# Fewer Strassen pairs in the second layer: two groups in 10 chunks, one group in 13, chosen by the chunk ahead

## The chip, the cores and the metric

One core of one Trainium2 chip runs the program. The metric is the device time of one execution in microseconds, the median of several executions. Lower is better.

## The reference, cut to what matters

For each of four batches an attention over channels gives a 256 x 256 matrix, which is multiplied with `v`; the 24320 rows that come out go through two dense layers with a squared ReLU between them. Only the second half matters for the change:

```
def _moe_ref(x, w_in, w_out):      # x: 24320 x 256, w_in: 256 x 2048, w_out: 2048 x 256
    h = x @ w_in
    r = np.maximum(h, 0.0)
    g = r * r
    return (g @ w_out).astype(np.float32)
```

## The kernel before, in words

**Tiling.** The attention matrix of a batch is folded into `w_in`, so the first layer takes `v` itself. The 6080 columns of a batch are cut into 6 chunks of 2 x 512 columns (the last of 2 x 480), 24 chunks in all. The 2048 hidden rows are 8 quads (`j` = 0 to 7): a quad is a 2 x 2 block of tiles, two halves of the hidden rows by two halves of the chunk's columns. Every value is split into a high and a low fp32r part, and a product is three matmuls (high-high, low-high, high-low).

**First layer.** A quad takes seven products (Strassen-Winograd), 21 matmuls into PSUM banks `h`, `x` and `z` (`product`, L624). ScalarE copies partial sums from bank to bank (`m1` L667, `m6` L676, `m7` L689) and VectorE adds (`plus_m7`, L694). `block` (L640 to L645) makes the squared ReLU of the tiles "11" and "12" and splits it; `blocks` (L654 to L656) does the same for "21" and "22" together.

**Second layer.** A quad that is not paired takes 8 units of three matmuls, 24 in all (`layer2`, L755). Two neighbouring quads 2g and 2g+1 (group g) can be taken as one pair by seven products. Two of these are in `pair_unit` (L799, 12 matmuls for the pair), and five in `pair_product` (L838, 30 matmuls): 42 in place of 48. For them VectorE makes sums of tiles (`right_op`, 8 instructions at L806), and ScalarE and VectorE split four of them into high and low (`pair_split`, L813 and L814), into the one buffer `th`. The tiles "12" of a paired quad are not split in `block`. The results are added up in four tiles `res`: the first pair of a chunk starts its PSUM bank afresh; a later one gets the sum so far copied into the bank ahead of it (`pair_seed`, L822), and where a chunk has two groups, every product of the first is copied out (L852).

**Which quads.** `SGS = (0, 2)` and `groups(ci)`: no group in chunk 0, groups 0 and 2 in chunks 1 to 22, group 0 in chunk 23: 45 pairs. The pair's products come 2.6 to 5.6 quads after its first quad, so those of group 2 end in the first two quads of the next chunk. The factors of the pairs lie in scratch memory (`wss`); they are made in chunk 0 (`decode_w_out`, `combine_w_out`) and loaded on the SP queue (`load_wss`, L202). Quads that aren't paired load `wo` (`load_wo`, L197).

**Side work.** While a batch's chunks run, the next batch's scores are computed (`score_norm`, `score_split`, `score_burst`, L256, about 0.8 pairs of tiles in a quad for 30 quads), then its softmax, then the folding of its attention matrix into `w_in` (`right7`, `fold7`, L482) and the split of the result (`combine`, L538 and L539), which is written to scratch memory (L541) and read back for each quad (`load_wt`, L547). This goes on in chunks 0 to 17. `combine` writes into a buffer of `wt` (three, shared with `load_wt`) or into `th`.

**Order.** Everything is emitted in an order written out by hand: `plan` lists 15 places in a quad, and `at(u, fn, ...)` puts a piece of side work at the time u, counted in quads. `pinned` holds side work behind certain copies and adds of the main work, and `high_priority` puts an instruction ahead on its engine. Each engine takes its instructions in that order.

Of the kernel before, what the change touches and what calls it, by code (L numbers as in the profile page):

```python
# [20 lines left out]
def tile_channel_attention_relu2_ffn(ctx, tc, kq, vT, tau, w_in, w_out, outT):  # L21
# [15 lines left out]
    nc = tc.nc  # L37
# [6 lines left out]
    NJ = DFF // P // 2  # L44
# [4 lines left out]
    G = 4  # L49
# [30 lines left out]
    K12, KS4, K11, KS2, KS3, K22, KS1 = range(NP)  # L80
# [1 line left out]
    wo = {}  # L82
    ws = {}
    wosc = {}
    SGS = (0, 2)
    wss = {g: scratch.tile([P, NP, 2, 2, P], F32, name=f"wss{g}") for g in SGS}
    wo32 = scratch.tile([P, 4, C], F32, name="wo32")

# [57 lines left out]
    def decode_w_out(g):  # L146
# [15 lines left out]
        for i in range(2):  # L162
# [3 lines left out]
            nc.gpsimd.dma_start(out=wosc[j], in_=w[i].bitcast(F32))  # L166
            if g in SGS:
                for k, f, e in ((K12, 1, 0), (K11, 0, 0), (K22, 1, 1)):
                    nc.gpsimd.dma_start(out=wss[g][:, k, i], in_=w[i][:, :, f, e].bitcast(F32))
        if g == 0:  # L170
            nc.gpsimd.dma_start(out=wo32, in_=W)
        elif g in SGS:
            win["out", g] = W
# [337 lines left out]
    def combine(b, g):  # L511

        if (b, g) not in parts:
            parts[b, g] = combine_parts(b, g)
        next(parts[b, g], None)

    def combine_parts(b, g):

        eng = nc.vector
        u = us.pop((b, g))  # L520
        S = work.tile([P, 4, GW], F32, name="sq", tag="sq")
        s2, s3, s1, s4 = (S[:, i] for i in range(4))
        eng.tensor_add(out=s1, in0=u[:, 0, 1], in1=u[:, 1, 1])
        eng.tensor_sub(out=s2, in0=s1, in1=u[:, 0, 0])
        eng.tensor_sub(out=s3, in0=u[:, 0, 0], in1=u[:, 0, 1])
        eng.tensor_sub(out=s4, in0=u[:, 1, 0], in1=s2)
        for i in range(2):
            j = 2 * g + i
            if i and b:
                yield  # L530
            if b and (g, i) in ((0, 1), (3, 0)):
                w = work.tile([P, 4 * HMAX], F32R, name="th", tag="th", bufs=1)
                w = w[:, :2 * NP * P].rearrange("p (l i c) -> p l i c", l=2, i=NP)
            else:
                w = work.tile([P, 2, NP, P], F32R, name="wt", bufs=WB)
            js = slice(i * P, (i + 1) * P)
            for o, x in ((w[:, :, 0:2], u[:, :, 0, js]), (w[:, :, 2:3], u[:, 1:2, 1, js]), (w[:, :, 3:7], S[:, :, js])):
                nc.scalar.copy(out=o[:, 0], in_=x)  # L538
                eng.tensor_sub(out=o[:, 1], in0=x, in1=o[:, 0])  # L539
            wsc[b, j] = scratch.tile([P, 2, NP, P], F32, name=f"wsc{j}", bufs=2)  # L540
            nc.gpsimd.dma_start(out=wsc[b, j], in_=w.bitcast(F32))  # L541
            if b == 0:
                wt[0, j] = w
# [8 lines left out]
    chunks = [(b, 2 * sum(widths[:i]), w) for b in range(B) for i, w in enumerate(widths)]  # L552
# [43 lines left out]
    state = {}  # L596
# [3 lines left out]
    raw2 = {}  # L600

    def groups(ci):
        return () if ci == 0 else SGS[:1] if ci == len(chunks) - 1 else SGS

    def paired(q):
        return q[1] // 2 in groups(q[0])
# [12 lines left out]
    def product(q, i, out, start):  # L619
        ci, j = q  # L620
        T = chunks[ci][2]
        w, v = wt[ci, j], vt[ci, i]
        for n, (l, r) in enumerate(((0, 0), (0, 1), (1, 0))):
            nc.tensor.matmul(out=out[:, :T], lhsT=w[:, l, i], rhs=v[:, r, :T], start=start and n == 0,  # L624
                             stop=n == 2, skip_group_check=True)

    def block(q, c, ps, eng):

        T = chunks[q[0]][2]
        split = not paired(q) or c == "11"  # L630
        if paired(q):
            p, i = (q[0], q[1] // 2), q[1] % 2
            raw, tag = (raw11, "raw11") if c == "11" else (raw12, "raw12")
            if i == 0:
                raw[p] = work.tile([P, 2, HMAX], F32, name=tag, tag=tag, bufs=1)
            r = raw[p][:, i, :T]
        else:
            r = work.tile([P, HMAX], F32, name="r", bufs=1)[:, :T]
        with tc.high_priority():
            nc.scalar.activation(out=r, in_=ps[:, :T], func=AF.Relu)  # L640
        nc.scalar.activation(out=r, in_=r, func=AF.Square)  # L641
        if split:
            hl = work.tile([P, 2, HMAX], F32R, name="g1", bufs=3)
            eng(out=hl[:, 0, :T], in_=r)  # L644
            nc.vector.tensor_sub(out=hl[:, 1, :T], in0=r, in1=hl[:, 0, :T])  # L645
            gs[q, c] = hl[:, 0], hl[:, 1]
# [31 lines left out]

    def m2(q):
        product(q, A12, state[q]["X"], False)  # L680
        block(q, "11", state[q]["X"], nc.scalar.copy if q[0] == 0 and q[1] < NJ - 1 else nc.vector.tensor_copy)

    def m7(q):
        T = chunks[q[0]][2]
# [100 lines left out]
    sums2 = {}  # L785
# [30 lines left out]
    PLACE = {K11: (0, 0), KS2: (1, 0), KS3: (0, 1), KS1: (1, 1)}  # L816
    seeds = {}

    def pair_seed(p, k):
        T = chunks[p[0]][2]  # L820
        seeds[p, k] = x = ps_x.tile([P, HMAX], F32, name="x")
        nc.scalar.copy(out=x[:, :T], in_=sums2[(p[0],) + PLACE[k]][:, :T])  # L822

    def pair_product(p, k):

# [61 lines left out]
    for kt in range(NT):  # L887
        g = kt // G
# [57 lines left out]
    def at(u, fn, *args):  # L946
        side.setdefault(round(u, 3), []).append((fn, args))
# [7 lines left out]
    for g in range(1, NG):  # L955
        u = 2 * (g - 1)
# [8 lines left out]
        at(u + 1.9, decode_w_out, g)  # L965
        if g in SGS:
            at(u + 2.6, combine_w_out, g)
# [7 lines left out]
    for b in range(1, B):  # L975
        u0 = (b - 1) * QB
        first, last = (NJ + 2 if b == 1 else 0), 30
        for i in range(NT // 2):
            u, k = u0 + first + i * (last - first) // (NT // 2), 2 * i
            if k % G == 0:  # L980
                at(u - (2.15 if b > 1 and k // G == 2 else 3.4), score_load, b, k // G)
            at(u - 0.8, score_norm, b, k)
            if b > 1 or k > LATE[-1]:
                at(u - 1.0, score_split, b, k)
                at(u - 0.5, score_split, b, k + 1)
                at(u + MID, score_burst, b, [k, k + 1])
        end = u0 + last
        at(end - 0.6, squares_split, b)
        at(end + MID, norms_wide, b)
        at(end + 1.6, lambda b=b: exps(b, s_acc[b]))  # L990
        at(end + 2 + MID, attnT, b)
        for g in range(0, NG, 2):
            u = end + 3 + 3.5 * g
            if b == 1:
                at(u - 3.5, load_wins2, g)
            for i in range(NP):
                at(u + i - (0.7 if b == 1 else 2.5), right7, b, g, i)
                at(u + i + MID, fold7, b, g, i)
            for i, du in enumerate(((0, 1.78, 2, 3.55), (0, 1.55, 2.78, 3.55))[g // 2]):
                at(u + NP + du, combine, b, g + i // 2)  # L1000
    for n, (ci, j) in enumerate(quads):
        if ci:
            at(n - 1.5, load_wt, ci, j)
            if not paired((ci, j)):
                at(n - (1.0 if j // 2 - 1 not in groups(ci) else 0.7 if j % 2 else 1.7), load_wo, ci, j)
            elif j % 2 == 0:
                p = ci, j // 2
                for u, *args in ((-1.1, K12, 2), (0.85, K11), (1.8, KS2), (2.8, K22), (3.75, KS3), (4.1, KS1)):
                    at(n + u, load_wss, p, *args)
                for u, k in ((1.1, KS3), (1.2, KS1), (1.75, KS2), (1.85, K22)):  # L1010
                    at(n + u, right_op, p, k, 0)
                for u, k in ((2.15, KS3), (2.25, KS1), (2.45, KS2), (2.8, K22)):
                    at(n + u, right_op, p, k, 1)
                for u, k in ((2.95, KS2), (3.7, K22), (4.05, KS3), (4.78, KS1)):
                    at(n + u, pair_split, p, k)
                for u, k in ((2.6, K11), (3.53, KS2), (3.93, K22), (4.6, KS3), (5.6, KS1)):
                    if p[1] and k != K22:
                        at(int(n + u) + 0.4, pair_seed, p, k)
                    at(n + u, pair_product, p, k)
        if j == 0 and ci:  # L1020
            at(n - NJ + (0.05 if ci > 1 else 1.0), load_v, ci)

            def start(ci=ci, n=n):
                for k, step in enumerate(v_combos(ci)):
                    at(n + (-3.2, -2.9, -2.4, -0.95, -0.85, -0.6, -0.55)[k], v_split, *step)
            at(n - 4.0, start)
# [23 lines left out]
    for n, q in enumerate(quads):  # L1050
        if paired(q) and q[1] % 2 == 0:
            a, b = quads[n - 2], quads[n - 1]
# [11 lines left out]
    for n in range(len(quads) + 1):  # L1064
        q = quads[n] if n < len(quads) else None
# [39 lines left out]
```

## Time and profile before

| | |
|---|---|
| median of 3 runs | 2178.41 us (2176.2 to 2179.84) |
| profiled execution, its own time | 2174.31 us |
| span of its instructions | 2172.5 us |
| TensorE matmul (PE) | 2129.8 us busy, 98%, 9622 matmuls |
| TensorE weight load (PEld) | 1735.9 us, 80% |
| VectorE (DVE) | 2005.1 us, 92% |
| ScalarE (ACT) | 1603.0 us, 74% |
| DMA | 482.88 MB, mean 222 GB/s |
| granted TensorE clock | 1.000 |

PE's busy time is modelled: matmuls overlap, and a matmul that starts a little late still leaves PE busy. The number of matmuls in a stretch, each with the time from one start to the next, tells more than the busy share.

### The profile page before, as it was taken

Reading aid. Unit: us, or ns where it says so; the run is one execution under the profiler, and the core shown is the slowest. Engines: PE = TensorE matmul, PEld = TensorE weight load, DVE = VectorE, ACT = ScalarE, POOL = GpSimd, SP = SyncE. Lnnn points to the kernel's source line nnn. Section 1 sums busy time; section 2 is a strip of 40 time slices with the busy share of each in tenths; the row PEclk is TensorE's granted clock in tenths of the full one; section 3 lists DMA queues with packets and bytes.
Section 4 is the critical chain, followed back from the end, with each engine's and each line's share of the span. In section 5 each row is a group of like instructions: output and inputs, shape, how many; then the busy total and the mean of one; then the engine's idle time right before and its main releaser. Section 6 shows DMA issues by size and latency. Waiting matters only on the chain.

```text
span 2172.5 us, 27874 instructions
## 1 busy us (share of the span) xinstructions
PE 2129.8 (98%) x9622; PEld 1735.9 (80%) x9622; DVE 2005.1 (92%) x2877; ACT 1603.0 (74%) x2628; POOL 97.5 (4%) x178
## 2 busy tenths in 40 slices
PE   9999999999999999999999999999999999999999
PEld 8887787878868788887887878887777788888888
DVE  7899999999999999998999999999899898988885
ACT  6888787767777777776777777877677677677674
POOL 0120000001000000000000000000000000000000
PEclk9999999999999999999999999999999999999999
DMA  9887746467776565556867656556675665565552
GB/s 369 333 290 282 269 174 220 153 238 250 275 266 233 200 208 194 184 190 211 282 236 267 232 189 222 174 196 199 211 263 207 254 205 170 190 220 175 180 190 89
DMA packets 122045, 482.88 MB, mean 222 GB/s; under 512 B 14192, under 2 KB 16880, under 8 KB 115120
## 3 DMA queue, kind: packets, MB, share of 16 engines
q1 hardware_dynamic: 105024, 409.97, 55.6%
q0 software_dynamic: 16880, 71.12, 8.2%
q8 instruction: 77, 1.26, 0.2%
q14 instruction: 64, 0.52, 0.1%
HBM read 408.95 MB, written 72.09 MB: 221 GB/s over the span
## 4 chain that ended last, share of the span: by engine, by line
PE 78%; issue 9%; ACT 6%; DVE 5%; DMA 2%; POOL 1%; SPq 0%; POOLq 0%; ACTq 0%
PE o L755 20%; PE h L624 19%; PE z L624 10%; PE x L838 10%; PE x L624 5%; PE o L799 4%; PE h L256 3%; PE o L838 3%; PE x L256 2%; PE o L256 1%; PE h L482 1%; DMA wt<-wsc 1%; ACT raw L640 1%; DVE g L656 1%; DVE raw L806 1%
## 5 line engine op out<-in xcount | busy, mean ns | idle before, releaser
L624 PE MATMUL h<-vt,wt 128*128 128x512 f32 (+1 forms) x2304 | 632.1, 390 | 15.0 <-DMA wt<-wsc 6.1
L755 PE MATMUL o<-g,wo 128*128 128x512 f32 (+1 forms) x2352 | 613.3, 389 | 3.0 <-DVE g L644 1.9
L624 PEld LDWEIGHTS h<-vt,wt 128*128 128x128 f32 x2304 | 428.5, 188 | 114.0 <-ACT x L667 11.8
L755 PEld LDWEIGHTS o<-g,wo 128*128 128x128 f32 x2352 | 437.3, 188 | 98.0 <-DVE g L656 4.2
L624 PE MATMUL z<-vt,wt 128*128 128x512 f32 (+1 forms) x1152 | 331.4, 393 | 3.3 <-ACT z L676 3.0
L806 DVE TENSOR_TENSOR raw<-raw,raw 128x512 f32<-128x512 f32 (+1 forms) x360 | 244.0, 679 | 25.8 <-ACT raw L641 23.8
L624 PEld LDWEIGHTS z<-vt,wt 128*128 128x128 f32 x1152 | 208.7, 188 | 55.7 <-ACT z L676 16.8
L813 ACT CAST th<-raw 128x1024 fp32r<-128x1024 f32 (+1 forms) x180 | 187.8, 1043 | 69.6 <-PE x L838 39.2
L814 DVE TENSOR_TENSOR th<-raw,th 128x1024 fp32r<-128x1024 f32 (+1 forms) x180 | 217.4, 1208 | 16.4 <-ACT th L813 15.7
L838 PE MATMUL x<-th,ws 128*128 128x512 f32 (+1 forms) x810 | 212.9, 393 | 3.9 <-ACT x L822 3.3
L852 ACT COPY res<-x 128x512 f32<-128x512 f32 (+1 forms) x111 | 64.8, 584 | 180.6 <-PE x L838 167.9
L838 PEld LDWEIGHTS x<-th,ws 128*128 128x128 f32 x810 | 148.3, 188 | 44.6 <-ACT x L822 10.9
L624 PE MATMUL x<-vt,wt 128*128 128x512 f32 (+1 forms) x576 | 162.2, 388 | 0.0
L799 PE MATMUL o<-g,wo 128*128 128x512 f32 (+1 forms) x540 | 156.9, 391 | 3.3 <-ACT g L655 3.3
L645 DVE TENSOR_TENSOR g<-r,g 128x512 fp32r<-128x512 f32 (+1 forms) x204 | 138.4, 678 | 13.5 <-ACT g L644 13.0
L656 DVE TENSOR_TENSOR g<-s,g 128x1024 fp32r<-128x1024 f32 (+1 forms) x102 | 123.4, 1210 | 24.8 <-ACT g L655 23.4
L676 ACT COPY z<-h 128x512 f32<-128x512 f32 (+1 forms) x192 | 111.0, 578 | 32.0 <-PE h L624 30.4
L667 ACT COPY x<-h 128x512 f32<-128x512 f32 (+1 forms) x192 | 110.7, 576 | 32.1 <-PE h L624 30.4
L641 ACT ACTIVATE r<-r 128x512 f32<-128x512 f32 (+1 forms) x204 | 128.7, 631 | 3.1
L624 PEld LDWEIGHTS x<-vt,wt 128*128 128x128 f32 x576 | 108.1, 188 | 22.1
L654 DVE SCALAR_TENSOR_TENSOR s<-s 128x1024 f32<-128x1024 f32 (+1 forms) x102 | 122.9, 1205 | 0.1
L656 DVE TENSOR_TENSOR g<-raw,g 128x1024 fp32r<-128x1024 f32 (+1 forms) x90 | 109.0, 1211 | 14.7 <-ACT g L655 14.3
(213 smaller groups left out, 3313.7 us busy)
## 6 DMA issues: line engine op xcount, KB each, us to landing
wt<-wsc SPq DMA_DIRECT2D x184, 896.0 KB, 5.4
ws<-wss SPq DMA_DIRECT2D x225, 256.0 KB, 2.8
kqt<-kq SPq DMA_DIRECT2D x47, 1024.0 KB, 7.2
wo<-wosc SPq DMA_DIRECT2D x94, 512.0 KB, 4.3
wsc<-wt POOLq DMA_DIRECT2D x26, 896.0 KB, 6.9
wo<-wss SPq DMA_DIRECT2D x45, 512.0 KB, 4.3
v<-vT SPq DMA_DIRECT2D x40, 512.0 KB, 5.6
outT<-res POOLq DMA_DIRECT2D x80, 256.0 KB, 5.4
```

The costliest lines, as they stand in the source:

```text
L256: ins = nc.tensor.matmul(out=s[:, h * C:(h + 1) * C], lhsT=l, rhs=r, start=first and h == 0 and n == 0, stop=last and n == len(terms) - 1, ...
L624: nc.tensor.matmul(out=out[:, :T], lhsT=w[:, l, i], rhs=v[:, r, :T], start=start and n == 0, stop=n == 2, skip_group_check=True)
L641: nc.scalar.activation(out=r, in_=r, func=AF.Square)
L645: nc.vector.tensor_sub(out=hl[:, 1, :T], in0=r, in1=hl[:, 0, :T])
L654: nc.vector.scalar_tensor_tensor(out=s, in0=s, scalar=0.0, op0=ALU.max, in1=s, op1=ALU.mult)
L656: nc.vector.tensor_sub(out=l, in0=s, in1=h)
L755: nc.tensor.matmul(out=ps[:, lo:hi], lhsT=w2[:, l, f, e], rhs=r[:, lo:hi], start=start and k == 0, stop=stop and k == 2, skip_group_check= ...
L799: nc.tensor.matmul(out=o[:, :T], lhsT=w[:, l], rhs=r[:, :T], start=first and i == 0, stop=False)
L806: op(out=x, in0=x, in1=y)
L813: nc.scalar.copy(out=h, in_=x)
L814: nc.vector.tensor_sub(out=l, in0=x, in1=h)
L838: nc.tensor.matmul(out=ps[:, :T], lhsT=w[:, l], rhs=r, start=fresh and i + n == 0, stop=k != K22 and i == 1 and n == 2, skip_group_check=n ...
```

## The change

Group 1 becomes possible beside 0 and 2. A list `TWICE` names ten chunks that keep groups 0 and 2 (1, 8, 9, 14, 15 and 18 to 22); a chunk right behind one of them that isn't in the list takes group 0 alone (2, 10, 16, 23), and the nine others take group 1 alone (3 to 7, 11 to 13, 17). Besides: in the first five chunks of `TWICE` the high part of tile "11" is cast on ScalarE in place of VectorE; `combine` puts the odd quad of every group into `th`, at times evenly spaced; seeds are for group 2 alone, earlier and with priority; one split and one product of a pair come 0.12 quads later; and one load of scores comes 1.25 quads sooner.

```diff
-    SGS = (0, 2)
+    SGS = (0, 1, 2)
+    TWICE = (1, 8, 9, 14, 15, *range(18, 23))
...
-            if b and (g, i) in ((0, 1), (3, 0)):
+            if b and i:
                 w = work.tile([P, 4 * HMAX], F32R, name="th", tag="th", bufs=1)
...
     def groups(ci):
-        return () if ci == 0 else SGS[:1] if ci == len(chunks) - 1 else SGS
+        return () if ci == 0 else (0, 2) if ci in TWICE else (0,) if ci - 1 in TWICE else (1,)
...
-        block(q, "11", state[q]["X"], nc.scalar.copy if q[0] == 0 and q[1] < NJ - 1 else nc.vector.tensor_copy)
+        block(q, "11", state[q]["X"], nc.scalar.copy if q[0] == 0 and q[1] < NJ - 1 or q[0] in TWICE[:5] else nc.vector.tensor_copy)
...
-        nc.scalar.copy(out=x[:, :T], in_=sums2[(p[0],) + PLACE[k]][:, :T])
+        with tc.high_priority():
+            nc.scalar.copy(out=x[:, :T], in_=sums2[(p[0],) + PLACE[k]][:, :T])
...
-                at(u - (2.15 if b > 1 and k // G == 2 else 3.4), score_load, b, k // G)
+                at(u - 3.4, score_load, b, k // G)
...
-            for i, du in enumerate(((0, 1.78, 2, 3.55), (0, 1.55, 2.78, 3.55))[g // 2]):
+            for i, du in enumerate(range(4)):
                 at(u + NP + du, combine, b, g + i // 2)
...
-                for u, k in ((2.95, KS2), (3.7, K22), (4.05, KS3), (4.78, KS1)):
+                for u, k in ((2.95, KS2), (3.7, K22), (4.17, KS3), (4.78, KS1)):
                     at(n + u, pair_split, p, k)
-                for u, k in ((2.6, K11), (3.53, KS2), (3.93, K22), (4.6, KS3), (5.6, KS1)):
-                    if p[1] and k != K22:
-                        at(int(n + u) + 0.4, pair_seed, p, k)
+                for u, k in ((2.6, K11), (3.53, KS2), (4.05, K22), (4.6, KS3), (5.6, KS1)):
+                    if p[1] == 2 and k != K22:
+                        at(int(n + u) + 0.34, pair_seed, p, k)
                     at(n + u, pair_product, p, k)
```

## Rows read from the trace of the kernel before

**Rows 1.** The page, busy time of each engine.
```profile
PE 2129.8 (98%) x9622; PEld 1735.9 (80%) x9622; DVE 2005.1 (92%) x2877; ACT 1603.0 (74%) x2628; POOL 97.5 (4%) x178
```

**Rows 2.** Windows: stretch, its length, each engine's busy us (count), clock, DMA, GB/s.
```profile
72.90:160.60 87.70, 87.11 (x378) 69.91 (x377) 83.40 (x127) 75.13 (x128) 22.54 (x37) 1.00 0.82 294
...
240.60:785.10 544.50, 528.56 (x2416) 427.96 (x2415) 528.61 (x768) 415.49 (x689) 25.39 (x46) 1.00 0.65 224
785.10:964.00 178.90, 178.31 (x841) 147.09 (x839) 172.62 (x239) 134.90 (x218) 4.32 (x8) 1.00 0.59 200
964.00:1325.00 361.00, 349.10 (x1592) 284.11 (x1593) 339.83 (x505) 269.44 (x453) 13.14 (x24) 1.00 0.66 230
...
1503.90:1678.30 174.40, 169.32 (x744) 136.76 (x745) 158.34 (x248) 122.86 (x214) 7.18 (x13) 1.00 0.64 219
1678.30:1761.00 82.70, 79.27 (x342) 62.62 (x341) 74.11 (x110) 59.11 (x101) 4.01 (x7) 1.00 0.66 237
1761.00:2081.40 320.40, 320.38 (x1394) 258.86 (x1392) 281.20 (x381) 228.46 (x369) 8.65 (x16) 1.00 0.58 190
```

**Rows 3.** The same windows, line L256 (score matmuls) alone: PE, PEld, clock, DMA.
```profile
240.60:785.10 544.50, 38.73 (x276) 36.95 (x276) 1.00 0.65 224
785.10:964.00 178.90, 18.07 (x132) 17.39 (x132) 1.00 0.59 200
964.00:1325.00 361.00, 22.27 (x156) 21.05 (x156) 1.00 0.66 230
```

**Rows 4.** Chain of waits (first row) and PE timeline: start us, us, what.
```profile
159.23 4.56 PE o L755 x20
...
812.18 1.24 PE L256 MATMUL h<-hl 128*128 128x256 f32 x9
813.25 0.86 PE L624 MATMUL z<-vt,wt 128*128 128x512 f32 x3
```

**Rows 5.** Groups of instructions by form, work of pairs and casts.
```profile
L806 DVE TENSOR_TENSOR raw<-raw,raw 128x512 f32<-128x512 f32 x304 | 207.6, 685 | 24.3 <-ACT raw L641 22.5
L814 DVE TENSOR_TENSOR th<-raw,th 128x1024 fp32r<-128x1024 f32 x152 | 185.2, 1218 | 11.0 <-ACT th L813 10.5
...
L813 ACT CAST th<-raw 128x1024 fp32r<-128x1024 f32 x152 | 159.9, 1052 | 45.3 <-PE x L838 34.8 <-DVE raw L806 5.8 <-PE o L838 2.4
...
L645 DVE TENSOR_TENSOR g<-r,g 128x512 fp32r<-128x512 f32 x168 | 115.0, 684 | 9.1 <-ACT g L644 8.8
...
L644 ACT CAST g<-r 128x512 fp32r<-128x512 f32 x91 | 56.8, 624 | 0.5
...
L822 ACT COPY x<-res 128x512 f32<-128x512 f32 x76 | 44.4, 584 | 0.0
...
L644 DVE CAST g<-r 128x512 fp32r<-128x512 f32 x77 | 32.3, 419 | 1.6 <-ACT r L641 1.0
```

**Rows 6.** Waits of the weight loads, whole span: us in total, times, longest us.
```profile
PEld x L838 <- ACT x L822: 13.3, 30, 1.1
PEld h L624 <- ACT x L667: 11.8, 20, 1.4
PEld h L256 <- ACT m L689: 9.7, 11, 1.6
...
PEld h L482 <- ACT m L689: 5.6, 4, 1.6
...
PEld h L624 <- DMA wt<-wsc: 2.2, 1, 2.2
```

**Rows 7.** Waits of the SP queue, whole span.
```profile
SPq L547 <- DMA wsc<-wt: 78.8, 15, 10.7
```

**Rows 8.** Groups by form in 72.9 to 160.6 us: `combine_w_out`, two groups.
```profile
L193 POOL DMA_DIRECT2D wss<-th x8 | 4.3, 548 | 9.0 <-DVE th L191 9.0
...
L191 DVE TENSOR_TENSOR th<-sq,th 128x1024 fp32r<-128x1024 f32 x2 | 2.4, 1215 | 0.0
...
L188 DVE TENSOR_TENSOR sq<-sq 128x256 f32<-128x256 f32 x2 | 0.8, 418 | 0.0
```

## The prediction

> **What bounds the kernel now.** I read the busy shares first, then windows of whole chunks, then the waits of the weight loads. By the shares [rows 1] PE is busy 98%, but that is modelled time, in which a late start hardly shows. So I counted matmuls. A run of 20 on 512 columns takes 4.56 us [rows 4], 0.228 us from start to start; nine on 256 columns start at 812.18 and the next kind at 813.25, 0.119 us each. For 480 columns I scale the first by 480/512, 0.214 us. A window's length less its matmuls at these prices is PE's **free time**, what a faster supply of operands can win at most.
>
> The windows begin at every eighth of the copies at L667 (the first of a chunk), and they are chosen by what the change does. It takes a pair away in chunks 2 to 7 (240.6 to 785.1 us), 10 to 13 (964.0 to 1325.0) and 16 to 17 (1503.9 to 1678.3). Each stretch holds one chunk of 480 columns, with 8 x 45 - 12 = 348 such matmuls. With [rows 2, 3]:
> - chunks 2 to 7: 2416 matmuls = 276 narrow (32.8 us) + 348 (74.5) + 1792 (408.6) = 515.9 of 544.5: 28.6 us free.
> - chunks 10 to 13: 156 (18.6) + 348 (74.5) + 1088 (248.1) = 341.2 of 361.0: 19.8 free.
> - chunks 16 to 17: 348 (74.5) + 396 (90.3) = 164.8 of 174.4: 9.6 free.
>
> Together 58.0 us in 12 chunks, 4.8 a chunk. Elsewhere there is little: chunks 8 to 9 come to 709 x 0.228 + 132 x 0.119 = 177.4 of 178.9, 0.75 a chunk (14 to 15 are nearly the same window), and chunks 19 to 22 to 1394 x 0.228 = 317.8 of 320.4, 0.65 a chunk. Chunk 18 has 82.7 - 342 x 0.228 = 4.7.
>
> VectorE is busy 97% of chunks 2 to 7, 94% of 10 to 13, 91% of 16 to 17, and 88% of 19 to 22 [rows 2]. So in the 12 chunks the bound is mostly two engines at once: PE holds the order, and VectorE (with ScalarE behind it, in one chain of copies, casts and subtractions) often delivers late. But chunks 8 to 9 run at 96% of VectorE with hardly any free time: the load alone doesn't make a wait, a burst does, as in the softmax, the folding and `combine`.
>
> **Part 1, what each pair taken away adds to PE.** Two quads take 48 matmuls in place of 42. Six at 0.228 are 1.37 us in nine chunks, six at 0.214 are 1.28 in three: 12.3 + 3.9 = **+16.2 us**, all on the engine that is the path. The Trainium skill, "TensorE: Matmul & The Clock Gate", section "Wait — 56ns, not 53.3ns?", gives 215.7 ns for 512 columns back to back, by which this term would be an estimated 15.3; the trace has 0.228 with a weight load before each matmul, and the measurement stands. The granted clock is 1.00, the 2.4 GHz level, in each stretch [rows 2], so nothing is to be had or lost there.
>
> **Part 2, what it takes off the others.** VectorE loses 8 sums at 0.685 and 4 subtractions at 1.218 and gains 2 splits of tile "12" at 0.684: 5.48 + 4.87 - 1.37 = 8.98 us a chunk, 108 us in all. ScalarE loses 4 casts at 1.052, 4 seeds and 4 copies out (as long as a seed, 0.584), and gains 2 casts at 0.624: 4.21 + 4.67 - 1.25 = 7.6 us a chunk [rows 5]. The adds into `res` stay at eight. VectorE then has 528.6 - 53.9 = 475 us of work in chunks 2 to 7 for 516 + 8 us of PE, 91%; 87% in 10 to 13 and 84% in 16 to 17. SP issues four loads fewer a chunk (six `ws` and `wo` of the pair go, two `wo` come).
>
> How much of the 58.0 goes? Nothing hides it: it is PE standing still. Lower end of what is left: the 0.65 to 0.75 a chunk of the calm stretches, 8 us. Upper end from the waits: those of the folding and the scores on a free bank `h` (L256 and L482 on L689) are 9.7 + 5.6 = 15.3 us [rows 6], and they belong to side work that stays; with the calm rate on top, 23. Nine of the 12 chunks hold softmax, folding or `combine`, but the queue in front of L689 gets shorter too, so I take 17 left, **-41.0 us**. What ends last then is PE itself, with its 0.228.
>
> **Part 3, chunk 0.** Group 1 needs its factors: four sums at 0.418 and one subtraction at 1.215, 2.9 us of VectorE, a cast of about that length on ScalarE, and ten DMAs on POOL at 0.55 [rows 8], which has 65 of 87.7 us idle. VectorE has 4.3 us idle in that chunk [rows 2], so the bounds are 0 and +4; nothing here can gain. I take **+1.5**. The factors are first read in chunk 3, long after.
>
> **Part 4, the cast moved to ScalarE** in 5 chunks, 40 quads: VectorE -0.419, ScalarE +0.624 each [rows 5], 16.8 and 25.0 us. ScalarE is at 75% in chunks 8 to 9, which covers it in the mean; queued behind it are the copies that free `h`, `x` and `z`, and PE waits for these. It can win what is free in the five chunks, some 4 us, and lose, if one quad in five has a copy 0.62 late, 5. I take 0.
>
> **Part 5, `combine` and `th`.** Odd quads go to `th` (12 times in place of 6), so `wt` has one more buffer free for `load_wt`. That load waits 78.8 us in all for `combine`'s writes [rows 7], and every load behind it on SP waits too; PE felt 2.2 us of it, in chunk 18 [rows 6]. In chunks with group 1 the splits use `th` only at quads 4.95 to 7.6, while `combine` has it at quads 0 to 3, so no clash. In chunk 18 the last `combine` takes `th` at quad 2.0, 0.22 later than before, and the first split wants it at 2.95: between -2 and +3 us. I take 0. **Seeds** (10 chunks keep them): PE waited 13.3 us for them in 22 chunks [rows 6]; the calm chunks have only 0.65 to win: -3 to 0, taken as 0. The shifts of 0.12 quads and the sooner load stay inside these ends.
>
> **Sum:** +16.2 - 41.0 + 1.5 = -23.3 us. The profiled execution took 2174.31 us (span 2172.5), 4.1 under the median, with nothing in it that the change would treat differently. Against the median: 2178.4 - 23.3 = **2155**.
>
> **Rivals.**
> - *All the free time goes* (VectorE was the whole cause): 8 or less is left, 16.2 + 1.5 - 50 = -32, to 16.2 - 58 = -42 where nothing is left; with chunk 18 mended some -45. That is 2134 to 2146, about 2140. For it: VectorE's load falls to that of chunks 19 to 22. Against: chunks 8 to 9 show that VectorE at 96% can go without waits. The Trainium skill, "Perfetto Trace Analysis", section "Identifying the Most-Contended Engine", takes the engine with the highest occupancy as the one to relieve, and leaves TensorE's matmul time out of it; by that rule VectorE's 92% decides, and this case is what it would give. The trace agrees on the share and not on the chunks.
> - *Given back:* some 20 us of the free time stays where it was or comes back as waits on casts and copies of the unpaired quads, whose tile "12" now passes both engines: 2174 to 2182, no change.
> - *Slower, PE alone is the bound:* the free time is made by the order (a bank `h` whose copy stands in ScalarE's queue behind side work) and not by the pairs; it stays, and the 72 matmuls come on top: up to +16 + 1.5, 2196. It decides from the point where over 44 of the 58 us stay, 3.7 a chunk. For it: chunk 18, at 90% of VectorE, has 4.7 free, and L256 and L482 wait for side work. Against: the waits on seeds and on L667 (13.3 and 11.8 us [rows 6]) hang on pairs, in chunks where the pair's sums, splits and copies stand in the same queues.
> - *The change doesn't do what it says:* 33 pairs must give 33 x 30 = 990 matmuls at L838, and 9694 in all. The diff's three cases of `groups` give 20 + 4 + 9 pairs, so I give this nothing of its own.
>
> **How the numbers follow.** Forecast (-12 to -32): 0.53, around 2155. All free time gone: 0.17. A smaller gain (-12 to -4.4): 0.09. Given back: 0.09. Slower: 0.12. A measurement of this kernel tells about 0.2%, 4.4 us, from no change: faster 0.79, same 0.09, slower 0.12. The range runs from 2136 (most of the first rival) to 2176 (small gains, half of "given back"), with about 0.05 left below and 0.15 above; the likeliest case alone has 2146 to 2166.
>
> **What would show it.** After the change the three stretches should hold 72 more matmuls and have 17 us free, 1.4 a chunk, by the same count; VectorE there near 85 to 91%; L806 at 264 instructions in place of 360; waits on L822 under 5 us; chunk 0 up to 4 us longer. Step 2 of the sum is wrong if the free time stays over 25 us or falls under 8; parts 3 to 5 are wrong if chunks 0, 1, 8, 9, 14, 15 or 18 differ by over 2 us each. The forecast as a whole falls if the waits on L689 and L667 stay as they are.

## The result, and the profile after

2139.74 us, median of 4 runs (2139.36 to 2140.38), against 2177.45 for the kernel before (median of 4 runs, the three of the table above and one more; 2176.2 to 2179.84): a ratio of 0.983 (95% interval 0.981 to 0.984), 37.7 us less. The span of the profiled execution fell from 2172.5 to 2138.1 us, by 34.4.

The page of the kernel after: engines, shares of the chain of waits, one group; then the shares of the chain before:

```profile
PE 2125.7 (99%) x9694; PEld 1757.7 (82%) x9694; DVE 1910.0 (89%) x2722; ACT 1547.7 (72%) x2549; POOL 102.7 (5%) x188
...
PE 92%; ACT 4%; DVE 3%; issue 1%; DMA 0%; POOL 0%; DVEq 0%; ACTq 0%; POOLq 0%
...
L807 DVE TENSOR_TENSOR raw<-raw,raw 128x512 f32<-128x512 f32 (+1 forms) x264 | 179.7, 684 | 28.3 <-ACT raw L642 25.8
```
```profile
PE 78%; issue 9%; ACT 6%; DVE 5%; DMA 2%; POOL 1%; SPq 0%; POOLq 0%; ACTq 0%
```

9694 matmuls are 72 more, and L807 (L806 before) has 264 instructions: 33 pairs. VectorE lost 95 us, ScalarE 55. PE's busy time [rows 1] hardly moved, although it does 72 matmuls more in 34 us less; it is the count against the length of the windows that tells. The windows are those of [rows 2], from the first copy of a chunk to that of another, then the score matmuls (L257, L256 before) in three of them:

```profile
72.80:161.70 88.90, 88.03 (x379) 69.71 (x378) 85.60 (x131) 75.76 (x128) 28.63 (x47) 1.00 0.86 305
240.20:769.90 529.70, 529.65 (x2478) 443.52 (x2477) 490.94 (x717) 381.68 (x634) 24.83 (x46) 1.00 0.63 224
769.90:942.80 172.90, 172.62 (x821) 143.39 (x820) 161.22 (x214) 139.37 (x228) 4.34 (x8) 1.00 0.59 197
942.80:1300.30 357.50, 354.84 (x1639) 294.66 (x1638) 318.53 (x474) 246.26 (x417) 13.06 (x24) 1.00 0.64 228
1300.30:1473.30 173.00, 172.71 (x821) 143.44 (x820) 161.28 (x214) 139.46 (x228) 4.34 (x8) 1.00 0.58 197
1473.30:1650.90 177.60, 174.96 (x775) 143.37 (x774) 150.95 (x236) 113.88 (x202) 7.09 (x13) 1.00 0.64 223
1650.90:1725.50 74.60, 74.32 (x324) 59.97 (x323) 67.78 (x101) 53.73 (x92) 3.80 (x7) 1.00 0.65 230
1725.50:2046.60 321.10, 320.44 (x1394) 258.99 (x1394) 280.90 (x381) 228.95 (x370) 8.68 (x16) 1.00 0.57 190
```
```profile
240.20:769.90 529.70, 37.14 (x276) 36.33 (x276) 1.00 0.63 224
769.90:942.80 172.90, 17.86 (x132) 17.55 (x132) 1.00 0.59 197
942.80:1300.30 357.50, 21.03 (x156) 20.61 (x156) 1.00 0.64 228
```

At the prediction's prices (0.228, 0.119 and 0.214 us, with 354 matmuls of 480 columns where a chunk with one pair has them), chunks 2 to 7 come to 529.8 of 529.7 us: **next to nothing free**, from 28.6. (By these prices 14 still narrower matmuls in chunks 2 to 7 count as wide ones, at most 3 us too much, before and after alike.) Chunks 10 to 13 have 357.5 - 351.7 = 5.8 left, 16 to 17 have 177.6 - 171.7 = 5.9. Most of that lies in chunks 10 and 16 alone; first the windows of these two, then three of the waits of PE's weight loads in chunk 10:

```profile
942.80:1038.50 95.70, 93.04 (x398) 73.09 (x397) 78.71 (x121) 59.09 (x101) 2.17 (x4) 1.00 0.58 196
1473.30:1569.00 95.70, 93.06 (x398) 73.03 (x397) 78.72 (x121) 59.03 (x100) 2.17 (x4) 1.00 0.59 195
```
```profile
PEld h L483 <- ACT m L690: 2.1, 2, 1.6
PEld h L625 <- ACT x L668: 1.4, 2, 0.9
PEld x L840 <- ACT x L824: 1.2, 1, 1.2
```

398 matmuls are 90.7 us of 95.7, so each of the two has 5.0 free. VectorE is only 82% busy there: this is the chunk with softmax and the first folding, where the products of group 2 of chunk 9 still end and group 0 begins. The waits of the weight loads over the whole span, beside [rows 6]; first the largest of the kernel before, which [rows 6] leave out, then those of the kernel after:

```profile
PEld z L624 <- ACT z L676: 16.8, 51, 1.1
```
```profile
PEld x L840 <- ACT x L824: 7.4, 14, 1.2
PEld h L625 <- ACT x L668: 6.1, 16, 0.9
PEld z L625 <- ACT z L677: 5.4, 22, 0.4
...
PEld h L483 <- ACT m L690: 4.2, 4, 1.6
```

The waits on the copy into bank `z` (L677, L676 before) fell from 16.8 to 5.4, those on seeds (L824) from 13.3 to 7.4, those on L668 from 11.8 to 6.1. Those of the folding on L690 fell from 5.6 to 4.2, and those of the score matmuls on it (9.7) are not listed any more.

### The profile page after: what moved, and what is told of

Same layout as the page of the kernel before. It is cut to its first block, busy times and chain, and to the rows that moved or that the text cites. A ratio compares the mean times of both kernels' runs of the same rounds, so it can differ in the third digit from the quotient of the medians.

```text
span 2138.1 us, 27570 instructions
## 1 busy us (share of the span) xinstructions
PE 2125.7 (99%) x9694; PEld 1757.7 (82%) x9694; DVE 1910.0 (89%) x2722; ACT 1547.7 (72%) x2549; POOL 102.7 (5%) x188
## 4 chain that ended last, share of the span: by engine, by line
PE 92%; ACT 4%; DVE 3%; issue 1%; DMA 0%; POOL 0%; DVEq 0%; ACTq 0%; POOLq 0%
PE o L756 30%; PE h L625 22%; PE z L625 11%; PE x L840 8%; PE x L625 5%; PE h L257 4%; PE o L800 3%; PE o L840 2%; PE x L257 2%; PE h L483 1%; DVE raw L807 1%; PE o L257 1%; ACT g L656 1%; ACT th L814 0%; ACT x L668 0%
## 5 line engine op out<-in xcount | busy, mean ns | idle before, releaser
L756 PEld LDWEIGHTS o<-g,wo 128*128 128x128 f32 x2928 | 546.3, 188 | 114.2 <-ACT g L656 3.6
L807 DVE TENSOR_TENSOR raw<-raw,raw 128x512 f32<-128x512 f32 (+1 forms) x264 | 179.7, 684 | 28.3 <-ACT raw L642 25.8
L646 DVE TENSOR_TENSOR g<-r,g 128x512 fp32r<-128x512 f32 (+1 forms) x252 | 171.6, 681 | 30.8 <-ACT g L645 28.9
L814 ACT CAST th<-raw 128x1024 fp32r<-128x1024 f32 (+1 forms) x132 | 138.4, 1049 | 76.0 <-PE x L840 53.8
L656 ACT CAST g<-s 128x1024 fp32r<-128x1024 f32 (+1 forms) x126 | 130.9, 1039 | 55.8 <-DVE s L655 55.7
L815 DVE TENSOR_TENSOR th<-raw,th 128x1024 fp32r<-128x1024 f32 (+1 forms) x132 | 160.1, 1213 | 11.7 <-ACT th L814 11.6
L840 PE MATMUL x<-th,ws 128*128 128x512 f32 (+1 forms) x594 | 153.9, 392 | 1.7 <-ACT x L824 1.5
L641 ACT ACTIVATE r<-z 128x512 f32<-128x512 f32 (+1 forms) x126 | 74.7, 593 | 108.2 <-PE z L625 86.9
L677 ACT COPY z<-h 128x512 f32<-128x512 f32 (+1 forms) x192 | 110.9, 578 | 37.4 <-PE h L625 36.6
L840 PEld LDWEIGHTS x<-th,ws 128*128 128x128 f32 x594 | 109.6, 188 | 30.6 <-ACT x L824 4.4
L668 ACT COPY x<-h 128x512 f32<-128x512 f32 (+1 forms) x192 | 110.7, 577 | 23.4 <-PE h L625 17.5
L237 DVE TENSOR_TENSOR aT<-aT,sq 128x1024 f32<-128x1024 f32 x92 | 112.4, 1222 | 16.8 <-ACT sq L236 14.4
```

The source lines that it names most:

```text
L656: nc.scalar.copy(out=h, in_=s)
L756: nc.tensor.matmul(out=ps[:, lo:hi], lhsT=w2[:, l, f, e], rhs=r[:, lo:hi], start=start and k == 0, stop=stop and k == 2, skip_group_check= ...
L807: op(out=x, in0=x, in1=y)
L814: nc.scalar.copy(out=h, in_=x)
L815: nc.vector.tensor_sub(out=l, in0=x, in1=h)
L840: nc.tensor.matmul(out=ps[:, :T], lhsT=w[:, l], rhs=r, start=fresh and i + n == 0, stop=k != K22 and i == 1 and n == 2, skip_group_check=n ...
```

## The experiments

Theory A: the pairs taken away freed PE. B: the small edits did. C: the place of a pair in its chunk decides. D: VectorE's mean load made the free time.

**Groups or edits.** `e1_groups_only` is the kernel before with

```diff
-    SGS = (0, 2)
+    SGS = (0, 1, 2)
+    TWICE = (1, 8, 9, 14, 15, *range(18, 23))
...
-        return () if ci == 0 else SGS[:1] if ci == len(chunks) - 1 else SGS
+        return () if ci == 0 else (0, 2) if ci in TWICE else (0,) if ci - 1 in TWICE else (1,)
...
-                    if p[1] and k != K22:
+                    if p[1] == 2 and k != K22:
```

> The kernel before with the new choice of groups alone (and the seeds for group 2 alone, which it needs); casts, th, times of combine, seeds and loads stay as they were. If the pairs taken away are what freed PE (theory A), nearly the whole gain stands: 2138 to 2150 us. If the small edits brought it (theory B), 2160 us or more.

Measured: 2138.88 us, ratio 0.982 (0.981 to 0.984). The groups are the whole gain; beside them, the small edits together are worth nothing that can be told. The other way round, `e2_edits_only`, the kernel after with the two lines of the groups undone:

```diff
-    SGS = (0, 1, 2)
+    SGS = (0, 2)
...
-        return () if ci == 0 else (0, 2) if ci in TWICE else (0,) if ci - 1 in TWICE else (1,)
+        return () if ci == 0 else SGS[:1] if ci == len(chunks) - 1 else SGS
```

> The kernel after with two pairs in chunks 1 to 22 as before; the small edits stay. Theory A: 2168 to 2180 us, as before, and 9622 matmuls. Theory B: below 2160 us.

Measured: 2234.50 us, ratio 1.027 (1.025 to 1.028): 57 us slower than before, which neither theory had. ScalarE's waits in it, then the chain of waits at one of the places, then PE's and ScalarE's timelines there:

```profile
ACT th L814 <- DMA wsc<-th: 46.5, 8, 7.8
```
```profile
644.50 10.41 DMA wsc<-th
...
654.99 0.07 ACT th L814
...
655.94 0.60 ACT r L641
...
656.56 0.58 ACT z L677
...
657.19 1.65 PE z L625 x3
```
```profile
649.75 0.93 PE L625 MATMUL h<-vt,wt 128*128 128x512 f32 x3
657.19 1.65 PE L625 MATMUL z<-vt,wt 128*128 128x512 f32 x3 [6.50 <-ACT z L677]
658.64 2.55 PE L257 MATMUL h<-hl 128*128 128x256 f32 x11
660.98 1.48 PE L756 MATMUL o<-g,wo 128*128 128x512 f32 x3
```
```profile
647.43 0.61 ACT L592 CAST vt<-v 128x512 fp32r<-128x512 f32 x1
654.99 1.04 ACT L814 CAST th<-raw 128x1024 fp32r<-128x1024 f32 x1 [6.95 <-DMA wsc<-th]
```

`combine` put its odd tile into `th`; the pair's split needs `th` and stands in ScalarE's queue until the tile is written out, 10.4 us after its issue; behind the split stands the copy L677, which PE needs. A write and three instructions of ScalarE in a row, and PE is idle 6.5 us. `e12_edits_but_th` takes back `combine`'s buffers and times alone:

```diff
-            if b and i:
+            if b and (g, i) in ((0, 1), (3, 0)):
...
-            for i, du in enumerate(range(4)):
+            for i, du in enumerate(((0, 1.78, 2, 3.55), (0, 1.55, 2.78, 3.55))[g // 2]):
```

> The kernel of e2_edits_only (two pairs in chunks 1 to 22 with the small edits, 2234.5 us) with combine's buffers and times as in the kernel before. If the one buffer th, held by combine's odd tiles until they are written, made all of its 57 us, 2170 to 2180 us. If the casts, seeds or shifts do harm beside two pairs, over 2190 us.

Measured: 2172.12 us, ratio 0.998 (0.997 to 0.999). So `combine`'s new buffers and times made all of the 57 us, and 5 more that the other edits give back; that it is the use of `th` is read from the waits above, since the run takes buffers and times back together.

**Number or place.** `e3_group0`:

```diff
-... (0,) if ci - 1 in TWICE else (1,)
+... (0,) if ci - 1 in TWICE else (0,)
```

> The kernel after with group 0 in place of group 1 in the nine chunks 3 to 7, 11 to 13, 17: the same 33 pairs and 9694 matmuls at an earlier place in the chunk. If the number of pairs decides (theory A), within 4 us of 2139.7. If the place decides (theory C: the pair's sums and splits must not fall on the quads in which softmax, folding and combine come), the free time in chunks 4 to 7, 11, 12 and 17 returns, 2 to 5 us each: 2150 to 2165 us.

Measured: 2193.02 us, ratio 1.007 (1.006 to 1.009): the same 9694 matmuls, 53 us slower than the kernel after. Again it is `th` first of all:

```profile
ACT th L814 <- DMA wsc<-th: 30.5, 6, 6.6
```

`e3b_group0_old_th` has the same edit on `e1_groups_only`, with `combine` as before.

> The kernel of e1_groups_only (2138.9 us: new choice of groups, all else as before) with group 0 in place of group 1 in the nine chunks. In e3_group0 the splits of the pair waited 30.5 us for the write of combine's tile in th; here combine takes th as before. If that buffer was all of the 53 us that e3_group0 lost, 2137 to 2145 us. If the place of the pair beside softmax, folding and combine costs by itself (theory C), 2150 us or more.

Measured: 2155.15 us, ratio 0.990 (0.989 to 0.992), 16 us over `e1_groups_only`. The two kernels, 38 us apart, differ in all the small edits; ScalarE's waits on `th` (30.5 and 7.2 us) put the difference down to that buffer, but no run shows it by itself. The rest isn't clean either. ScalarE's waits on `th`, and its timeline and PE's at the worst place, chunk 6:

```profile
ACT th L814 <- DMA wsc<-th: 7.2, 3, 3.4
```
```profile
627.77 1.04 ACT L814 CAST th<-raw 128x1024 fp32r<-128x1024 f32 x1 [3.02 <-DMA wsc<-th]
```
```profile
629.97 1.65 PE L625 MATMUL z<-vt,wt 128*128 128x512 f32 x3 [2.65 <-ACT z L677]
```

The old `combine` still puts one tile into `th` little more than a quad ahead of group 0's first split (at 1.78 and 2.95 in chunk 6). So theory C holds as far as this: a pair that wants `th` before `combine`'s tile is written out costs time. How much place costs without that buffer can't be read from this run.

**Chunks 10 and 16.** `e8_8_14`, the kernel after with

```diff
-    TWICE = (1, 8, 9, 14, 15, *range(18, 23))
+    TWICE = (1, 8, 14, *range(18, 23))
+    CASTS = (1, 8, 9, 14, 15)
...
-... or q[0] in TWICE[:5] else nc.vector.tensor_copy)
+... or q[0] in CASTS else nc.vector.tensor_copy)
```

> The kernel after with chunks 9 and 15 taken out of the list of two pairs, so that 9 and 15 take group 0 and 10 and 16 group 1; casts stay where they were. Two pairs fewer add 2 x 1.37 = 2.7 us of matmuls. If the 6 us that are free in each of chunks 10 and 16 come from the end of group 2 of the chunk before and from group 0, both beside softmax and folding (theory C), some 10 us go and the time is 2130 to 2135 us. If the softmax and folding make them alone, 2141 to 2144 us.

Measured: 2129.76 us, ratio 0.978 (0.977 to 0.980), 10 us less with 12 matmuls more. Windows of chunks 9 and 10 in it, then all waits of PE's weight loads in chunk 10:

```profile
854.40:947.30 92.90, 92.64 (x432) 76.88 (x431) 80.38 (x107) 67.56 (x110) 2.16 (x4) 1.00 0.52 179
947.30:1032.70 85.40, 85.40 (x380) 70.52 (x380) 72.32 (x112) 55.54 (x97) 2.16 (x4) 1.00 0.64 218
```
```profile
PEld h L626 <- ACT sq L395: 0.2, 1, 0.2
PEld o L757 <- DVE g L658: 0.2, 1, 0.2
```

The 380 matmuls at 0.228 us come to 86.6, over the window's 85.4: nothing is free in chunk 10, and the count can be some 1 us too high in a chunk. The 2.1 us wait of the folding on L690 is gone: with chunk 10's pair in the middle of the chunk and no end of a group 2 ahead of it, softmax and folding don't stop PE.

**Is PE the bound now?** `e5_no_pair`:

```diff
-... (0,) if ci - 1 in TWICE else (1,)
+... (0,) if ci - 1 in TWICE else ()
```

> The kernel after with no pair in the nine chunks that have group 1: 54 matmuls more, 6 x 1.37 + 3 x 1.28 = 12.1 us. There are only 2.8 us free in these chunks in the kernel after. If PE is the bound there now (theory A), 2149 to 2152 us. If a pair still costs more than it saves (VectorE still decides), under 2145 us.

Measured: 2149.29 us, ratio 0.987 (0.986 to 0.989): +9.6 us, where the 54 matmuls are priced at 12.1 and the expectation had 2.8 us free for them. A pair now pays in these chunks at about four fifths of its price in matmuls.

**VectorE: load, or what it does when?** `e7_dve_load` adds work to the kernel after; `e9_no_sums` leaves the eight sums of each pair out of the kernel before.

```diff
+    def load_dve():
+        nc.vector.tensor_mul(out=ones, in0=ones, in1=ones)
+
+    for n, (ci, j) in enumerate(quads):
+        if groups(ci) == (1,):
+            for k in range(2):
+                at(n + 0.2 + 0.5 * k, load_dve)
```

> The kernel after with two idle multiplications of 128 columns on VectorE in each quad of the nine chunks with group 1 (a constant tile times itself, result unchanged), an estimated 0.28 us each, 4.5 us a chunk: VectorE's share there goes from 0.89 to 0.96 up to 0.94 to over 1. If VectorE's mean load made the free time before (theory D), it returns: over 15 us, 2155 us or more. If bursts and buffers of the pair made it, only what exceeds 100% comes on top: 2140 to 2147 us.

Measured: 2141.01 us, ratio 0.983 (0.982 to 0.985), +1.3. The instructions took 0.287 us each (144 of them, 41 us). Two of the chunks, 3 and 6, in which VectorE is busy 95% and 99%:

```profile
330.30:425.00 94.70, 94.70 (x461) 79.91 (x460) 89.86 (x141) 67.56 (x112) 2.17 (x4) 1.00 0.54 187
...
590.80:680.70 89.90, 89.90 (x435) 75.04 (x434) 88.58 (x142) 64.47 (x108) 3.80 (x7) 1.00 0.69 246
```

The record of PE has no idle time in either. Theory D falls: at about the share that chunks 2 to 7 had before (97%), evenly spread and with nothing waiting for the added results, VectorE doesn't hold PE up.

```diff
-        op(out=x, in0=x, in1=y)
+        pass
```

> The kernel before without the eight sums of tiles of each pair (right_op left out, so the pairs' products take unsummed tiles): 45 pairs, the same 9622 matmuls, splits, casts, seeds, copies and loads, 240 us less of VectorE. If VectorE's work for the pairs made the free time (theory D), some 45 us go: 2125 to 2140 us. If ScalarE's part, the one buffer th and the seeds made it, 2160 us or more.

Measured: 2132.19 us, ratio 0.980 (0.978 to 0.981), 45 us less than before with the same 9622 matmuls:

```profile
PE 2114.0 (99%) x9622; PEld 1740.5 (82%) x9622; DVE 1802.1 (85%) x2517; ACT 1592.9 (75%) x2628; POOL 97.2 (5%) x178
```

Its windows of the same three stretches, then the wait of the folding in it:

```profile
240.00:763.60 523.60, 520.76 (x2414) 429.24 (x2413) 475.56 (x672) 412.41 (x688) 25.07 (x46) 1.00 0.66 232
941.70:1291.40 349.70, 345.76 (x1594) 284.86 (x1593) 303.93 (x440) 266.68 (x450) 13.21 (x24) 1.00 0.68 238
1469.60:1639.80 170.20, 167.44 (x743) 136.81 (x742) 140.55 (x215) 120.66 (x212) 7.23 (x13) 1.00 0.68 233
```
```profile
PEld h L482 <- ACT m L689: 4.7, 3, 1.6
```

At the same prices 8.2, 8.2 and 5.7 us are free in them, 22 of the 58. So the pairs' sums cost PE some 36 of the 58 us before; the kernel after, with 11.6 free, wins some 10 more, which is put down to what else goes with a pair (splits, seeds, copies, `th`); no run separates these. The waits of the score matmuls on L689 are gone with the sums alone.

Yet VectorE just as full with evenly spaced work doesn't cost PE its time. That points to when the work comes (a pair's sums, splits and adds fall within a few quads) or to what waits for it (the splits and products wait for the sums, nothing for the added multiplications). A run that keeps the pairs and spreads their sums wasn't made; that the bunching is the cause is inferred, not shown.

**The edits one by one.** `e4_cast_dve` takes back the casts (`or q[0] in TWICE[:5]` deleted), `e6_th_old` the two edits of `combine` (the diff of `e12_edits_but_th` on the kernel after).

> The kernel after with the casts of chunks 1, 8, 9, 14, 15 back on VectorE. By the free time of the chunks in e1_groups_only (2.3 in chunk 9 against 1.06, 1.0 in chunk 8 against 0.64, 1.1 in chunk 1 against 0.82), the moved casts are worth some 3.5 us: 2142 to 2145 us. If they are worth nothing, as the prediction had it, 2139 to 2141 us.

Measured: 2143.16 us, ratio 0.985 (0.983 to 0.986): the casts are worth 3.4 us.

> The kernel after with combine's buffers and times as in the kernel before. By chunks 10 and 16 (4.2 us free in e1_groups_only, 6.0 in the kernel after) the new ones cost 1.8 us each there: 2135 to 2138 us. If they mend a wait on the wt buffers instead, 2141 us or more.

Measured: 2138.61 us, ratio 0.983 (0.981 to 0.984): `combine`'s new buffers and times cost 1.1 us by the medians and nothing by the ratios (both 0.983): no more than the runs can tell.

`e11_best` is `e8_8_14` with the seeds as before:

```diff
-        with tc.high_priority():
+        if True:
...
-                        at(int(n + u) + 0.34, pair_seed, p, k)
+                        at(int(n + u) + 0.4, pair_seed, p, k)
```

> The kernel of e8_8_14 (two pairs in 1, 8, 14 and 18 to 22; 2129.8 us) with the seeds where they stood before, without priority. Chunks 19 to 22 have 0.85 to 0.92 us free with those and 1.14 with the new ones, so some 1 us less: 2128 to 2130 us, faster than both kernels.

Measured: 2128.37 us, ratio 0.978 (0.977 to 0.979), the fastest of all, 11.4 us under the kernel after. Against `e8_8_14` its 1.4 us lie inside the intervals.

## Why the prediction was right or wrong

The direction and the range (2136 to 2176) held; the likeliest case (2146 to 2166, around 2155) did not. The time came out where the first rival had it, about 2140; the range held because it took that rival in, not because the sum was near.

By the steps of the sum, with the windows above:

| step | forecast | found in the spans |
|---|---|---|
| part 1, 72 matmuls | +16.2 | +16.2 at the same price |
| part 2, free time in the 12 chunks | -41.0 | 58.0 to 11.6: -46.4 |
| part 3, chunk 0 | +1.5 | 87.7 to 88.9: +1.2 |
| parts 4 and 5, chunks 8 to 9 and 14 to 15 | 0 | 1.5 to 0.1 and 1.5 to 0.2: -2.7 |
| part 5, chunk 18 | 0 | 4.7 to 0.7: -4.0 |
| part 5, chunks 19 to 22 | 0 | 2.6 to 3.3: +0.7 |

This comes to -35.0 beside a span shorter by 34.4. The other 3 us of the 37.7 between the medians are where the profiled execution of before stood: 2174.31, 3.1 under the median of four.

**Part 1 was right** in the number of matmuls; from the other side, `e5_no_pair` pays 9.6 us for 54 of them, priced at 12.1. Where they would lie was wrong: not 72 but 140 more (62, 47 and 31) came into the three stretches, mostly products of group 2 of chunks 7, 13 and 17, which used to end in chunks 8, 14 and 18 (20, 20 and 18 fewer there).

**Part 2 was the right term, undersized:** it forecast 17 us left of the 58, and 11.6 are left. "I take 17 left" came from 15.3 us of waits by the scores and the folding on L689, which "belong to side work that stays". The side work stayed and most of those waits went, 4.2 of 15.3 are listed after. Those of the scores hung on the pairs' sums (`e9_no_sums`), those of the folding in chunk 10 on the pairs beside it (`e8_8_14`). The largest wait before, 16.8 us in all on the copy into `z`, was not looked at; it fell to 5.4. What did stay, 10 of the 11.6 us, is in two chunks, 10 and 16, for a reason the prediction didn't name: the end of group 2 of the chunk before, and group 0, beside softmax and folding.

**Part 5 on chunk 18** failed. It looked at `th` and `wt` in chunk 18 and overlooked that chunk 17 with group 1 sends no products into it (324 matmuls against 342 [rows 2]). The groups alone do it: `e1_groups_only`, with `th` as before, has 74.8 us there:

```profile
1650.70:1725.50 74.80, 74.80 (x326) 59.61 (x325) 69.05 (x103) 55.43 (x97) 4.01 (x7) 1.00 0.65 229
```

On the seeds it allowed -3 to 0; chunks 19 to 22 got 0.7 longer, too little to tell. On `th`, "no clash" for group 1 was right: ScalarE's splits wait 0.2 us for `combine`'s tile in the whole kernel after, and 30.5 with group 0 in the same chunks (`e3_group0`):

```profile
ACT th L814 <- DMA wsc<-th: 0.2, 1, 0.2
```

**Part 4** took 0 and got -3.4 (`e4_cast_dve`), inside its bounds.

**The signs.** L807 has its 264 instructions, and the 11.6 us lie between the 8 and 25 named for step 2. The waits on L824 were to be under 5 us and are 7.4. VectorE is busy 93%, 89% and 85% of the three stretches, for 91%, 87% and 84%: its busy time fell by 95 us, where parts 2 to 4 come to 108 + 17 - 3 = 122.

**The rivals.** "All the free time goes" gave the right time with a cause that only half stands: the pairs' sums on VectorE were most of it (`e9_no_sums`, 36 of 58 us), VectorE's share was not (`e7_dve_load`). The rule of the Trainium skill, "Perfetto Trace Analysis", section "Identifying the Most-Contended Engine", pointed at the right engine here; chunks with the same occupancy and no free time, before and in `e7_dve_load`, show that the share alone doesn't tell. "Slower" and "given back" fell: PE took what the others let go, 92% of the chain of waits in place of 78%.

## What to carry to other kernels

Count matmuls against the length of a window; a busy share of 98% hid 58 us in 12 chunks. A trick that saves work on the bound engine by adding work on another (here 1.37 us of matmuls for some 9 us of VectorE) is to be judged chunk by chunk, by what else runs there and which buffers both want, and not by mean occupancy. Whoever gives a single buffer a second user should look at what stands behind the one that waits for it: here a copy that TensorE needs.

## What was not expected of the hardware

In `e2_edits_only` the granted clock fell where PE had stood still. Four windows around the wait of 6.5 us:

```profile
640.00:650.00 10.00, 9.17 (x37) 6.31 (x36) 9.64 (x17) 4.96 (x8) 1.62 (x3) 1.00 0.77 254
650.00:657.00 7.00, 0.69 (x3) 0.21 (x2) 2.88 (x4) 1.98 (x3) 0.00 (x0) 0.68 1.03 429
657.00:664.00 7.00, 6.81 (x24) 5.95 (x25) 2.95 (x5) 4.46 (x8) 0.00 (x0) 0.59 0.13 53
664.00:671.00 7.00, 7.00 (x32) 5.74 (x31) 6.29 (x9) 4.72 (x8) 0.00 (x0) 1.00 0.47 150
```

Before it the clock was at the 2.4 GHz level (1.00); while PE stood still and in the 7 us after it the mean was 0.68 and 0.59, partly the 1.2 GHz level; then 1.00 again. After the wait PE did 24 matmuls in 7 us, and 32 in the next 7; by the timeline above, 11 on 256 columns take from 658.64 to 660.98, 0.21 us each in place of 0.119. So this wait cost more than itself, and that is part of the 57 us.
